# Centring x ahead of its transposes and applying its scale to the hidden sums, in a Fourier-mixing and MLP kernel

## The chip, the cores and the metric

The kernel runs on one core of a Trainium2 chip. The metric is the device time of one execution in microseconds (us), the median of several runs.

## What is computed

For x of 2048 rows (tokens) by 640 columns, a normalization and two branches that are summed with x:

```python
xn = layernorm(x)                                # over the 640 columns, eps 1e-5
a = xn @ dft_hid_re.T ; b = xn @ dft_hid_im.T    # 640 x 640
y = dft_seq_re @ a - dft_seq_im @ b              # 2048 x 2048
h = gelu(xn @ w1 + b1)                           # 640 -> 1536, tanh form
out = x + y + h @ w2 + b2                        # 1536 -> 640
```

All in float32. TensorE multiplies in a rounded float32 (`fp32r`), so each operand is split into a high part (rounded, by ScalarE) and a low part (the rest, by VectorE), and a product is three matmuls: high x high, high x low, low x high.

## The kernel before

The tokens are handled in four blocks of 512. The MLP of block 0 comes first, then that of blocks 1 and 2 together, then block 3, then the Fourier branch for all blocks. The order of each engine's instructions is written out by hand: the program's order is the queue's order on every engine, and each instruction waits only for the data and the places that it needs.

**The head** (lines 647 to 755). Four loads bring block 0's rows, a chunk of 128 rows each, into `row_places`. Meanwhile TensorE runs `NWARM` = 19 matmuls on zeros (line 666). The three tiles `warm` that they read have the places of the first three chunks of w1 (tag `w1r`), so a load of w1 waits until the warming matmuls on its tile are done: `NGATE` = (7, 10) says that the first tile is read by 7 of them, the second by 3, the third by the rest. Each chunk of x gets its mean and variance (chunk 1 on ScalarE, the others by `ln_stats` on VectorE), the reciprocal root by a Sqrt on ScalarE and a Newton step on VectorE (lines 690 to 713), and is normalized into `xp`: chunks 0 and 1 by ScalarE, 2 and 3 by VectorE in two parts. Then 20 transposes on TensorE (line 682) put block 0, transposed, in five PSUM banks, and five splits (line 736) make `XT`. With `XT` and the first w1 chunk's split the hidden sums of unit 0 start (line 320). `FIRST` is the order of unit 0's 15 matmuls.

**The units of block 0** (loop at line 1157). The 1536 hidden columns are 12 units of 128. `hidden(g)` is 15 matmuls that sum unit g in a PSUM bank, `unit` (line 332) its gelu on ScalarE, `split_unit` its split into `hs`, `output(g)` 15 matmuls that add its share to the output's five banks. Iteration i splits w1's chunk i+3 and w2's chunk i+1 (`prep_w1`, `prep_w2`; high on ScalarE, then low on VectorE), issues the loads of later chunks into the places so freed (three places each), then does `background(i)`, `hidden(i+2)`, `gelu(i+2)`, `late(i)` and `output(i)`. So TensorE's order is hidden(2), output(0), hidden(3), output(1) and so on.

**The rows beside the units.** Later stages need the normalized rows in other layouts. `background`, `late` and `normalize_a` compute statistics of blocks 1 and 2, normalize their rows in place on VectorE (`ln_apply`, line 231), and move them: `put_rows` writes them to DRAM (`xn`), `put_z` turns them around into `Z["b"]` (block 2, in the tile that `xp` had) and `Z["a"]` (block 1, in the place of block 0's rows), each by 16 DMAs; those of `Z["a"]` are all issued by POOL. `make_forms` then transposes parts of Z on VectorE and splits them. Loads are issued by SP in order. ScalarE's Sqrt and Gelu are in different tables, so a table load stands between them.

The lines that the change and the prediction speak of:

```python
W1[0], first_w1 = slots[1, 0], w1r.pop(0)...             # 722
nc.scalar.activation(W1[0][:, 0], first_w1, AF.Copy)      # 723
for i in range(NF - 2):                                   # 1157
    prep_w1(i + 3)
    if i == 3: normalize_a()
    prep_w2(i + 1)
    load_w1(i + 6); load_w2(i + 4)
    background(i)
    acc = hidden(i + 2)
    gelu(i + 2, acc)
    late(i)
    output(i)
```

Of the kernel before, what the change touches and what calls it, by code (L numbers as in the profile page):

```python
# [10 lines left out]
F32 = mybir.dt.float32  # L11
# [8 lines left out]
NWARM = 19  # L20
NGATE = (7, 10)
# [5 lines left out]
def kernel(  # L27
# [105 lines left out]
    ident = early.tile([P, P], F32, name="ident")  # L133
    es_r = ExitStack()
# [41 lines left out]
    def split(hi, lo, src, perm=False):  # L176
# [6 lines left out]
        low(l, s, h)  # L183
# [26 lines left out]
    def ln_stats(c):  # L210
        m = MV
# [6 lines left out]
    def ln_scale(n):  # L218

        m = MV[:, :n]  # L220
        ve, r, t = m[:, :, 2], m[:, :, 3], m[:, :, 4]
        nc.scalar.activation(r, m[:, :, 1], AF.Sqrt, bias=eps[:, 0:1])
        nc.vector.tensor_scalar(ve, m[:, :, 1], EPS, None, op0=ALU.add)
        nc.vector.reciprocal(r, r)
        nc.vector.scalar_tensor_tensor(t, r, -0.5, r, op0=ALU.mult, op1=ALU.mult)
        nc.vector.tensor_tensor(t, t, ve, op=ALU.mult)
        nc.vector.scalar_tensor_tensor(r, t, 1.5, r, op0=ALU.add, op1=ALU.mult)

    def ln_apply(c, eng=nc.vector):
        m = MV[:, slot[c]]  # L230
        eng.tensor_scalar(xt[c], xt[c], m[:, 0:1], m[:, 3:4], op0=ALU.subtract, op1=ALU.mult)

    def ln_apply_chunked(dst, c, j0=0, j1=ND):

        m = MV[:, slot[c]]
# [51 lines left out]
    def prep_w1(i, n=None):  # L287
        if i < NF:
            W1[i] = slots[1, i]
            split(W1[i][:, 0], W1[i][:, 1], w1r.pop(i if n is None else n).rearrange("p a b -> p (a b)"))  # L290

    def prep_w2(i):
        if i < NF:
            W2[i] = slots[2, i]
            split(W2[i][:, 0], W2[i][:, 1], w2r.pop(i), perm=True)
# [36 lines left out]
    def unit(g, acc, plus=None, a=None):  # L332
# [4 lines left out]
        if plus is not None:  # L337
            add(a, plus, acc)
            acc = a
        nc.scalar.activation(a, acc, AF.Gelu_apprx_tanh, bias=b1c[:, i : i + 1])  # L340
# [10 lines left out]
    FIRST = [(0, 0), (0, 2), (1, 0), (1, 2), (0, 1), (2, 0), (2, 2), (1, 1), (3, 0), (3, 2)]  # L351
    FIRST += [(2, 1), (4, 0), (4, 2), (3, 1), (4, 1)]
# [327 lines left out]
    def transpose_x(c, j0, j1):  # L680
# [5 lines left out]
    last = 1  # L686
    f, m = MV[:, 0], MV[:, last]
    root, step, shift = f[:, 3:4], f[:, 4:5], f[:, 5:6]
    ln_stats(0)
    nc.scalar.activation(root, f[:, 1:2], AF.Sqrt, bias=eps[:, 0:1])  # L690
    scratch = mr.tile([P, 2 * TB], F32, tag="hs", bufs=3, name="scratch")[:, :D]
    nc.scalar.activation(scratch, xt[last], AF.Copy, scale=-1.0 / D, accum_out=m[:, 5:6])
    nc.scalar.activation(
        chunked(xp[:, last]),
        xt[last].rearrange("p (q c i) -> p q c i", q=Q, i=B),
        AF.Identity,
        bias=m[:, 5:6],
    )
# [1058 lines left out]
```

## Time and profile before

| | |
|---|---|
| median of 3 runs | 851.65 us (851.21 to 852.05) |
| span of the profiled execution | 849.9 us |
| TensorE, matmuls | busy 841.9 us, 99% of the span, 3711 |
| VectorE | busy 686.7 us, 81% |
| ScalarE | busy 368.6 us, 43% |
| GpSimd | busy 67.7 us, 8% |
| the chain of work that ended last | TensorE 98%, DMA 1% |
| DMA | 166.53 MB, mean 196 GB/s |

The span runs from the first to the last instruction of one execution taken by the hardware profiler; the page states no other time for that execution. The timed runs lie around it: their median is 1.75 us above the span. In the rows below, PE is TensorE's matmuls, PEld its weight loads, DVE VectorE, ACT ScalarE, POOL GpSimd, and SPq the queue on which SP issues DMAs. A timeline row has the start in us, the duration in us, the engine, the source line, the operation, what is written and read, the shapes, and how many instructions are merged in the row; in brackets, how long the engine was idle before it and what ended the wait. A row of the chain has start, duration, engine, tile and line.

### The profile page before, as it was taken

The page shows a single profiled execution, that of the slowest core. Times are in us where ns is not written, and L with a number is a line of the kernel's source. Part 1 is how long each engine was busy: PE and PEld are TensorE (multiplying, and loading weights), DVE is VectorE, ACT ScalarE, POOL GpSimd, SP SyncE. Part 2 cuts the span into 40 slices and gives each one's busy share as a digit, 9 for nine tenths or more (in the row PEclk, how much of TensorE's full clock was granted, in tenths as well). Part 3 has the DMA queues.
Part 4 walks back from the last instruction along what each step waited for, and adds up shares of the span by engine and source line. Part 5 has one row for each costly group of instructions (what it writes and reads, how often), then busy time and mean ns, then how long its engine had stood idle before and what let it go on. Part 6 is the DMA issues. An engine that isn't in the chain of part 4 may idle for free.

```text
span 849.9 us, 10599 instructions
## 1 busy us (share of the span) xinstructions
PE 841.9 (99%) x3711; PEld 696.7 (82%) x3711; DVE 686.7 (81%) x909; ACT 368.6 (43%) x527; POOL 67.7 (8%) x116
## 2 busy tenths in 40 slices
PE   8999999999999999999999999999999999999997
PEld 7888888888888888888888888888888888888886
DVE  7979889767844778979978887889967998885687
ACT  7655666654453555443444344232323433323241
POOL 0440024222301000000000000000000000000002
PEclk9999999999999999999999999999999999999999
DMA  8995667878977897958744679763745799705464
GB/s 230 288 248 158 139 163 250 260 223 305 262 192 199 333 323 138 209 120 193 158 137 107 167 220 283 165 144 99 214 150 156 229 237 234 303 19 180 124 172 108
DMA packets 199141, 166.53 MB, mean 196 GB/s; under 512 B 61648, under 2 KB 170192, under 8 KB 198576
## 3 DMA queue, kind: packets, MB, share of 16 engines
q1 hardware_dynamic: 188320, 140.42, 62.7%
q0 software_dynamic: 7600, 24.91, 8.7%
q10 hardware_dynamic: 3168, 0.52, 0.3%
q8 instruction: 29, 0.48, 0.2%
q14 instruction: 24, 0.20, 0.1%
HBM read 115.75 MB, written 46.14 MB: 190 GB/s over the span
## 4 chain that ended last, share of the span: by engine, by line
PE 98%; DMA 1%; DVE 0%; ACT 0%; SPq 0%; issue 0%; ACTq 0%
PE banks L301 29%; PE banks L302 29%; PE banks L300 29%; PE banks L320 10%; DMA row<-in_A_x_dram 1%; PE banks L682 0%; DVE st L215 0%; ACT xp L714 0%; SPq L208 0%; DVE yo L1722 0%; DVE mv L216 0%; ACT mv L707 0%; DVE mv L708 0%; ACTq L707 0%
## 5 line engine op out<-in xcount | busy, mean ns | idle before, releaser
L186 ACT ACTIVATE as<-r 128x1024 fp32r<-128x1024 f32 x80 | 85.0, 1062 | 171.1 <-PE banks L302 150.4
L300 PE MATMUL banks<-as,xab 128*128 128x512 f32 x407 | 158.3, 389 | 0.0
L302 PE MATMUL banks<-as,xab 128*128 128x512 f32 x407 | 158.3, 389 | 0.0
L301 PE MATMUL banks<-as,xab 128*128 128x512 f32 x407 | 158.3, 389 | 0.0
L189 DVE TENSOR_TENSOR as<-r,as 128x1024 fp32r<-128x1024 f32 x80 | 97.2, 1215 | 38.1 <-ACT as L186 38.0
L301 PEld LDWEIGHTS banks<-as,xab 128*128 128x128 f32 x407 | 76.4, 188 | 15.9
L302 PEld LDWEIGHTS banks<-as,xab 128*128 128x128 f32 x407 | 76.4, 188 | 15.8
L300 PEld LDWEIGHTS banks<-as,xab 128*128 128x128 f32 x407 | 76.4, 188 | 15.8
L300 PE MATMUL banks<-as,xc 128*128 128x512 f32 x224 | 87.1, 389 | 0.0
L301 PE MATMUL banks<-as,xc 128*128 128x512 f32 x224 | 87.1, 389 | 0.0
L302 PE MATMUL banks<-as,xc 128*128 128x512 f32 x224 | 87.1, 389 | 0.0
L186 ACT ACTIVATE as<-rt 128x1024 fp32r<-128x1024 f32 x32 | 34.0, 1063 | 72.5 <-PE banks L302 57.9
L320 PE MATMUL banks<-xt,xab 128*128 128x512 f32 x240 | 56.8, 390 | 0.0
L189 DVE TENSOR_TENSOR hs<-ab,hs 128x512 fp32r<-128x512 f32 x36 | 24.7, 685 | 37.6 <-ACT hs L186 37.6
L320 PEld LDWEIGHTS banks<-xt,xab 128*128 128x128 f32 x240 | 45.0, 188 | 9.4
L301 PEld LDWEIGHTS banks<-as,xc 128*128 128x128 f32 x224 | 42.1, 188 | 8.8
L302 PEld LDWEIGHTS banks<-as,xc 128*128 128x128 f32 x224 | 42.0, 188 | 8.7
L300 PEld LDWEIGHTS banks<-as,xc 128*128 128x128 f32 x224 | 42.1, 188 | 8.7
L1280 POOL DMA_DIRECT2D out_dram<-u x4 | 2.6, 658 | 568.8 <-DVE u L463 568.8
L302 PE MATMUL banks<-hs,xc 128*128 128x512 f32 x120 | 46.7, 389 | 0.0
L300 PE MATMUL banks<-hs,xc 128*128 128x512 f32 x120 | 46.7, 389 | 0.0
L301 PE MATMUL banks<-hs,xc 128*128 128x512 f32 x120 | 46.7, 389 | 0.0
(240 smaller groups left out, 1678.9 us busy)
## 6 DMA issues: line engine op xcount, KB each, us to landing
raw<-in_A_dft_seq_re_dram SPq DMA_DIRECT2D x64, 256.0 KB, 5.4
raw<-in_A_dft_seq_im_dram SPq DMA_DIRECT2D x64, 256.0 KB, 5.1
w1r<-in_B_w_dram SPq DMA_DIRECT2D x144, 80.0 KB, 3.5
wit<-wst POOLq DMA_DIRECT2D x15, 384.0 KB, 4.2
wit<-wst POOLq DMA_DIRECT2D x20, 256.0 KB, 4.5
forms_ab<-xab SPq DMA_DIRECT2D x4, 1280.0 KB, 7.7
xab<-wit SPq DMA_DIRECT2D x13, 384.0 KB, 4.5
row<-xn SPq DMA_DIRECT2D x14, 320.0 KB, 5.3
```

Source lines behind the costliest of these rows:

```text
L186: nc.scalar.activation(h, s, AF.Copy)
L189: nc.vector.tensor_tensor(l, s, h.bitcast(F32), op=ALU.subtract)
L300: nc.tensor.matmul(acc, wh, mh, start=first, stop=False, skip_group_check=goes_on)
L301: nc.tensor.matmul(acc, wh, ml, start=False, stop=False, skip_group_check=goes_on)
L302: nc.tensor.matmul(acc, wl, mh, start=False, stop=last, skip_group_check=goes_on)
L320: nc.tensor.matmul(acc, W1[i][:, a, j * P : (j + 1) * P], XT[j][:, b], start=n == 0, stop=n == len(steps) - 1)
L1280: queues[q % len(queues)].dma_start(rows_of(out, t)[:, :, q * DQ + c0 : q * DQ + c1], src[q * B : (q + 1) * B])
```

## The change

Four things are done.

- The head: chunks of block 0 are only centred before the transposes (chunks 0, 2 and part of 3 on VectorE by `centre`, chunk 1 and part of 3 on ScalarE by `centre_beside`). Their scale (the reciprocal root) is computed behind the splits of `XT`. Four more transposes on TensorE spread the scale of each token over all partitions (bank 0), and ScalarE copies it to a tile `scale`. The gelu of each of the first 12 units is preceded by a product of the sums with `scale` on VectorE. 14 warming matmuls are left, with gates at 6 and 9, and the first w1 chunk's high part goes to VectorE.
- The rows of block 0 are scaled into `row_places` by ScalarE (`rows_beside`), those of block 2 normalized by ScalarE (`ln_apply_beside`).
- The low parts of w1's and w2's chunks are kept back (`rest`) and issued in `beside_split`, between the high and the low part of unit i+2's own split; the loads into the places that they free follow there, ahead of the normalization and the moves of the rows.
- Block 1 gets its statistics (in tile `MVA`) and normalization one iteration earlier, and the backgrounds from iteration 4 on stand behind the gelu; those of 6 and later move up by one or part of one.

```diff
-NWARM = 19
-NGATE = (7, 10)
+NWARM = 14
+NGATE = (6, 9)
...
+    def roots(m):
+        nc.scalar.activation(m[:, :, 3], m[:, :, 1], AF.Sqrt, bias=eps[:, 0:1])
...
+    def ln_apply_beside(c):
+        m = (MVA if 4 <= c < 8 else MV)[:, slot[c]]
+        nc.scalar.activation(xt[c], xt[c], AF.Identity, bias=m[:, 5:6], scale=m[:, 3:4])
...
+        if g < NF:
+            add(a, acc, scale, ALU.mult)
+            acc = a
         nc.scalar.activation(a, acc, AF.Gelu_apprx_tanh, bias=b1c[:, i : i + 1])
...
     ln_stats(0)
-    nc.scalar.activation(root, f[:, 1:2], AF.Sqrt, bias=eps[:, 0:1])
...
+    centre(0)
+    mean_beside(1)
+    centre_beside(1)
+    spread_beside(1)
+    ln_stats(2)
+    centre(2, 0, 2)
+    mean_beside(3)
+    centre(2, 2, ND)
+    nc.vector.tensor_scalar(MV[:, 3, 0:1], MV[:, 3, 5:6], -1.0, None, op0=ALU.mult)
+    centre_beside(3, 0, 2)
+    centre(3, 2, ND)
     transpose_x(0, 0, ND)
+    transpose_x(1, 0, ND)
     transpose_x(2, 0, 2)
     transpose_x(3, 0, 2)
-    transpose_x(last, 0, ND)
     transpose_x(2, 2, ND)
-    transpose_x(3, 2, ND - 1)
+    transpose_x(3, 2, ND)
+    W1[0], first_w1 = slots[1, 0], w1r.pop(0).rearrange("p a b -> p (a b)")
+    nc.vector.tensor_copy(W1[0][:, 0], first_w1)
...
-    acc0 = hidden(0, slice(1, None))
+    acc0 = hidden(0, slice(0, 14))
     prep_w1(1)
-    acc1 = hidden(1)
+    spread_beside(3)
+    v, r, t = MV[:, :, 1], MV[:, :, 3], MV[:, :, 4]
+    nc.scalar.activation(r, v, AF.Sqrt, bias=eps[:, 0:1])
...
+    prep_w1(2)
     prep_w2(0)
-    prep_w1(2)
+    acc1 = hidden(1, slice(0, 2))
+    hidden(0, slice(14, None))
+    hidden(1, slice(2, 6))
+    for c in range(NC):
+        nc.tensor.transpose(bank(0)[:, c * P : (c + 1) * P], MV[:, c, 3:4].to_broadcast([P, P]), ident)
+    hidden(1, slice(6, None))
+    scale = rows.tile([P, TB], F32, tag="yt", bufs=2, name="scale")
+    nc.scalar.activation(scale, bank(0), AF.Copy)
...
+    def beside_split(i, lows):
+
+        if i == 1:
+            ln_scale_table(MV)
+            ln_shift()
+        for f in lows:
+            f()
+        if i + 6 < NF + 3:
+            load_w1(i + 6)
+        load_w2(i + 4)
+        if i == 1:
             Z["b"] = zo_tile("z_b")
             for c in range(2 * NC, 3 * NC):
-                ln_apply(c)
+                ln_apply_beside(c)
             put_z(Z["b"], A["rows_b"], nc.gpsimd, nc.sync)
             put_rows(2, A["rows_b"])
         if i == 2:
-            ln_stats(6)
-            ln_stats(7)
+            ln_scale_table(MVA)
+            Z["a"] = as_z(row_places)
+            for c in range(NC, 2 * NC):
+                ln_apply(c)
+            put_z(Z["a"], A["rows_a"], nc.gpsimd)
...
     for i in range(NF - 2):
-        prep_w1(i + 3)
-        if i == 3:
-            normalize_a()
+        lows = []
+        prep_w1(i + 3, rest=lows)
...
-        prep_w2(i + 1)
-        if i + 6 < NF + 3:
-            load_w1(i + 6)
-        load_w2(i + 4)
-        background(i)
+        prep_w2(i + 1, lows)
+        rows_beside(i)
+        if i < 4:
+            background(i)
         acc = hidden(i + 2)
...
-        gelu(i + 2, acc)
+        gelu(i + 2, acc, lambda k: beside_split(i, lows) if k else None)
+        if i >= 4:
+            background(i)
         late(i)
         output(i)
```

In `background`, what stood under iteration 6 (moves of block 1's rows, the forms `ua0`, `ua1`, `va0`, a difference in `Z["b"]`) stands under 5, `oa0` and `va1` under 6 instead of 7, the next difference and two transposes under 7 instead of 8, and the loads of x's rows for block 0's output and of b2 under 9 instead of 8.

More of the change, by code (lines that the diff above doesn't have):

```diff
@@ L133 @@
     ident = early.tile([P, P], F32, name="ident")
+    MVA = early.tile([P, 4, 6], F32, name="mva")
     es_r = ExitStack()
@@ L182, in split @@
         high(h, s)
-        low(l, s, h)
+        if rest is None:
+            low(l, s, h)
+        else:
+            rest.append(lambda: low(l, s, h))
     def high(h, s):
```

154 lines of the change are left out of this document (74 added, 80 removed).

## The prediction

> **What bounds the kernel now.** I read the page first (busy shares), then the chain of work that ended last, then the timeline of the first 25 us engine by engine, and last the timeline and the waits of 25 to 70 us.
>
> ```profile
> PE 841.9 (99%) x3711; PEld 696.7 (82%) x3711; DVE 686.7 (81%) x909; ACT 368.6 (43%) x527; POOL 67.7 (8%) x116
> ```
>
> ```profile
> 9.71 2.27 PE banks L682 x19
> ...
> 12.32 10.07 PE banks L320 x44
> 22.39 0.23 PE banks L300
> ...
> 25.79 3.40 PE banks L320 x15
> ...
> 32.59 3.40 PE banks L320 x15
> ```
>
> The span is 849.9 us and TensorE is busy for 841.9 of it. From 9.71 us to the output's last steps the chain holds nothing but matmuls: one unit of the MLP (15 matmuls of the hidden sums, 15 of the output) takes 32.59 - 25.79 = 6.80 us, or 0.227 us a matmul, and none waits. So the loop cannot get shorter by other engines' work; only its start can move. The most that can be won is in front of 9.71; all that can be lost is a new wait.
>
> ```profile
> 1.92 7.05 PE L666 MATMUL banks<-warm 128*128 128x512 f32 x19 [1.92 <-DVE warm L657]
> 9.71 2.27 PE L682 MATMUL banks<-ident,xp 128*128 128x128 f32 x19 [0.73 <-ACT xp L714]
> 11.73 0.48 PE L320 MATMUL banks<-xt,xab 128*128 128x512 f32 x1
> 12.04 0.27 PE L682 MATMUL banks<-ident,xp 128*128 128x128 f32 x1
> 12.07 10.32 PE L320 MATMUL banks<-xt,xab 128*128 128x512 f32 x44
> 22.23 0.39 PE L300 MATMUL banks<-hs,xc 128*128 128x512 f32 x1
> ```
>
> Nineteen warming matmuls, 20 transposes of x, 45 hidden matmuls, and the first output matmul at 22.23. **That last time is the one I forecast**; behind it the order of TensorE is unchanged.
>
> **The change, part by part. 1: the head.** The transposes no longer wait for the roots, only for the means.
>
> ```profile
> 4.66 0.21 DVE L216 BATCH_NORM_AGGREGATE mv<-st 128x2 f32<-128x12 f32 x1
> 5.10 0.72 ACT L692 ACTIVATE scratch<-row 128x640 f32<-128x640 f32 x1
> 5.73 0.18 ACT L692 ACTIVATION_READ_ACCUMULATOR scratch<-row 128x1 f32 x1
> 5.95 0.83 ACT L693 ACTIVATE xp<-row,mv 128x640 f32<-128x640 f32 x1
> 6.81 0.74 ACT L699 ACTIVATE scratch<-xp 128x640 f32<-128x640 f32 x1
> 7.28 0.83 DVE L215 BATCH_NORM_STATS2 st<-row 128x6 f32<-128x320 f32 x2
> 9.60 1.51 DVE L236 TENSOR_SCALAR xp<-row,mv 128x256 f32<-128x256 f32 x4
> 11.03 2.56 ACT L186 ACTIVATE xt<-banks 128x512 fp32r<-128x512 f32 x5
> 11.83 3.07 DVE L189 TENSOR_TENSOR xt<-banks,xt 128x512 fp32r<-128x512 f32 x5
> ...
> 14.82 0.81 DVE L189 TENSOR_TENSOR xab<-w1r,xab 128x640 fp32r<-128x640 f32 x1
> ```
>
> Chunk 0: its statistics end at 4.87 as now. Centring is the instruction of L236 with one operand less; four halves took 1.51, so a whole chunk about 0.6 (bounds 0.4 and 0.82, the pass over two tensors at 14.82): ready 5.5. Chunk 1: ScalarE no longer does the root first, so it starts when the chunk lands, by 5.10 at the latest; I take 4.7. Mean, centring and spread take 0.85 + 0.86 + 0.8 and end at about 7.2. Chunk 3 has landed by 7.28, since its statistics start then; its mean on ScalarE ends at 8.0 to 8.1, two of its five blocks are centred there in 0.5 (between two fifths of L693's 0.83 and the whole) by 8.5, the rest on VectorE by 8.8. Now TensorE:
>
> ```profile
> 2.51 0.63 PE L666 MATMUL banks<-warm 128*128 128x512 f32 x1
> ...
> 4.22 0.63 PE L666 MATMUL banks<-warm 128*128 128x512 f32 x1
> 4.65 0.63 PE L666 MATMUL banks<-warm 128*128 128x512 f32 x1
> ...
> 7.19 0.62 PE L666 MATMUL banks<-warm 128*128 128x512 f32 x2
> 7.43 0.62 PE L666 MATMUL banks<-warm 128*128 128x512 f32 x2
> 7.65 0.63 PE L666 MATMUL banks<-warm 128*128 128x512 f32 x2
> ...
> 10.72 0.38 PE L682 MATMUL banks<-ident,xp 128*128 128x128 f32 x2
> ```
>
> The warming matmuls start 0.43 apart up to the 13th at 7.19 (eleven steps behind the second, at 2.51) and 0.23 apart after it: there the clock doubles, although the column of the granted clock reads 1.00 throughout. The 14th of them starts at 7.43, so the first transpose can follow at 7.66. At 0.11 each (the 10th of the 19 started at 10.72, about 1.0 behind the first) the 20 transposes run to 9.86, none of them waiting: the 13th, the first of chunk 3, is due at 8.98 with its data ready at 8.5. The present one of that kind started at 10.72, and the split of block 0 on ScalarE followed at 11.03, the first hidden matmul at 11.73: 1.01 behind the transpose. So the first hidden matmul comes at 8.98 + 1.01 = **10.0 instead of 11.73**.
>
> The first chunk of w1 must be there:
>
> ```profile
> 5.31 5.60 SPq L278 DMA_DIRECT2D w1r<-in_B_w_dram  x12
> ```
>
> ```profile
> w1r<-in_B_w_dram SPq DMA_DIRECT2D x4, 80.0 KB, 2.1
> ```
>
> Its first load waits for the gate's 7th warming matmul (4.65 + 0.63 = 5.28); with the 6th it is issued 0.43 earlier, at 4.88. Four issues at about 0.45 and 2.1 to 2.2 to land (the second row, the loads issued from 6.3 to 8) give 8.4. VectorE, free at 8.7, rounds it (0.5; bounds 0.4 and 0.82, as for the centring) and takes the low part (0.82) by 10.1: in time for the third matmul.
>
> From 10.0 to the first output matmul: 45 matmuls x 0.227 = 10.2; a wait of 0.25 at the second, since its block is split 0.48 after the first (L186); four transposes of the scale, 0.44 at the 0.11 of L682 (bounds 0.44 and 0.9, if a broadcast operand streams at half speed); and 0.19 that today's 10.50 us holds beyond its 45 matmuls and its one visible transpose. Together 21.1. **The head gives 22.23 - 21.1 = 1.15 us.**
>
> The four scale transposes wait for the roots of all chunks. Behind the splits of x ScalarE does w1's next high part, chunk 3's spread and one root (to 13.5), VectorE a low part and four small steps (to 14.6); TensorE gets there at 15.2. Nothing waits. The copy of the scale ends at 16.4.
>
> **2: the units.** Each of the first 12 gets one more VectorE pass, and the low parts of the next weights go behind it. The weights' low part used to be done an iteration ahead; now it starts only when the hidden sums before it end, and is needed 3.40 + 0.45 us later.
>
> ```profile
> 16.95 0.69 ACT L340 ACTIVATE ab<-banks,b1c 128x512 f32<-128x512 f32 x1
> 17.68 0.63 ACT L186 ACTIVATE hs<-ab 128x512 fp32r<-128x512 f32 x1
> 24.84 8.23 SPq L278 DMA_DIRECT2D w1r<-in_B_w_dram  x8
> 30.60 1.28 ACT L222 ACT_TABLE_LOAD   x1
> 42.95 2.18 DVE L231 TENSOR_SCALAR rt<-rt,mv 128x640 f32<-128x640 f32 x4
> ```
>
> ```profile
> L463 DVE TENSOR_TENSOR ab<-ab,banks 128x512 f32<-128x512 f32 x7 | 4.8, 684 | 3.8 <-PE banks L302 3.8
> ```
>
> The product costs 0.68, in sequence 0.61 (L189's five in 3.07); 12 of them are 7.3 us of VectorE, against four row passes (2.2, the row at 42.95) that go to ScalarE at L693's 0.83 or 0.75 in sequence. A chunk's statistics take 0.83 + 0.21, a high part of weights 0.63 in sequence, as L692's pass of 640 columns. With hidden(3) starting at 21.1 + 3.4 = 24.5, the nearest points are:
> - hidden(3): ScalarE from 16.4: table 1.3, two units 2.6, so VectorE splits unit 1 until 21.0; two statistics (2.1), product 0.61, low part 0.82: 24.5 plus 0.15 to reach TensorE, needed at 24.95. Spare 0.3.
> - hidden(5): ScalarE adds two weight pairs (2.5), four rows (3.0), unit 2 (1.3), two tables and two roots (2.9), unit 3 (1.4): 31.4. VectorE then splits unit 3 (to 32.1), four statistics to 36.2, product and low part to 37.7; needed at 38.55. Spare 0.7. Behind it two further low and small steps and four row passes end at 41.3.
> - hidden(9): next.
>
> Each costs nothing while spared; an error of half a microsecond in such a sum costs TensorE that half, once. The loads of w1 and w2 wait for these low parts, which end later in the unit than now; but SP is at earlier loads until 33.1 (the row at 24.84) when the low part that frees the next place ends at about 31, so I price that at nothing. Without the cover such a load would land some 2 us later, and it is used three units, 20 us, after its issue.
>
> **3: the rows' moves.** Block 1's rows are normalized by 41.3, and POOL moves them.
>
> ```profile
> 45.43 3.81 POOL L762 DMA_DIRECT2D row<-rt  x7 [2.76 <-DVE rt L231]
> ```
>
> ```profile
> 62.69 1.30 DVE L259 STREAM_TRANSPOSE ztua<-row 128x512 f32<-128x512 f32 x2 [1.05 <-DMA row<-rt]
> ...
> 67.98 0.69 DVE L189 TENSOR_TENSOR hs<-ab,hs 128x512 fp32r<-128x512 f32 x1
> ```
>
> Now the rows are done at 45.13, POOL issues from 45.43, VectorE waits for the landing until 62.69, 17.26 behind the first issue, and is free again 5.29 later, at 67.98. The forms stand one iteration earlier after the change, in front of the product and the low part for hidden(9). That matmul group starts at 24.5 + 6 x 6.8 = 65.3, its low part is needed at 65.6: landing + 5.29 + 0.61 + 0.82 = landing + 6.72, so the rows must land by **58.9**. First issue at 41.6 and the same 17.26 give 58.9: no wait, and no spare.
>
> **Sum:** 1.15 won, nothing lost: the span 849.9 becomes 848.75. The median of the timed runs, 851.65, lies 1.75 above the span; carried over, **850.5 us**.
>
> **The rivals.**
> *A, the rows land late.* Each microsecond beyond 58.9 is a microsecond of TensorE. For it: 16 issues on POOL overlap block 2's moves more than now. Against: they start 3.8 earlier. If they land no earlier than now, at 62.69, hidden(9) waits 3.8, and the time is 850.5 + 3.8 = 854.3. From 60.05 on the gain is gone. This is the case on the slower side. Chance 0.15.
> *B, the clock.* The clock doubled 5.27 us behind the first matmul (1.92 to 7.19), and 14 at 0.43 last only 6.0. If in an execution the doubling comes later and the transposes do not bring it, the 20 transposes take 4.4 instead of 2.2, and up to 12 hidden matmuls 0.2 more each: 1.15 turns into a loss of 0.3 + 2.2 + 2.4 - 1.15 = 3.75, 855.4; if it comes half-way, 0.4 to 1.2 are lost and the time is 850.9 to 851.7. The present rows only show the clock kept through 2.3 us of transposes, not raised by them. Chance 0.08 for the whole, 0.12 for half. The Trainium skill speaks for B: its page "TensorE: Matmul & The Clock Gate" says in "Part 4: PE-mode transpose" that transposes do not count as busy time for the clock, and in Part 1 that the activity window is free-running, so the doubling moves between executions.
> *C, small waits.* A third to one microsecond lost in hidden(3) to hidden(5), where 0.3 to 0.7 is spared, or in a first w1 chunk that lands at 9.5 instead of 8.4 (0.5): 850.8 to 851.5. Chance 0.25.
> *D, more than forecast.* If the clock doubles early, the transposes wait for chunk 3 alone (8.6), the first hidden matmul comes at 9.65: 850.1. Nothing in front of 9.71 offers more, so over 0.2% (1.7 us) is nearly excluded.
>
> **How the numbers follow.** Forecast 0.40 (with D), A 0.15, B 0.20, C 0.25. The range leaves out the far parts of A (0.05), B whole (0.08) and the end of D (0.06): 849.9 to 853.0. Faster by over 0.2% means below 849.95: 0.07, D at its end. Slower means above 853.35: A from 61.75 on and B whole, 0.15. Within 0.2%, about what a measurement of this kernel can tell: 0.78.
>
> **What would show it.** The first hidden matmul at 10.0 and the first output matmul at 21.1; four transposes there without a wait in front; no idle TensorE at hidden(3), (5) and (9); the first transpose of block 1's form at 58.9 or sooner; warming matmuls whose spacing halves before the 14th. An idle TensorE behind 25 us names A or C, transposes 0.22 apart name B.

## The result and the profile after

| | before | changed |
|---|---|---|
| median | 851.61 us (851.21 to 852.19, 12 runs) | 853.21 us (851.64 to 857.39, 12 runs) |
| span of the profiled execution | 849.9 us | 850.1 us |
| time of that execution | about 852.0 us (span and 2.1) | 852.21 us |

The ratio is 1.0026, with a 95% interval of 1.0013 to 1.0038: the changed kernel is slower by a quarter of a per cent, and its executions spread over 5.8 us where before's spread over 1. The profiled executions whose time is known lie 1.9 to 2.2 us above their spans, most of them 2.1. The execution profiled is one of the faster ones, so its trace shows the cause, but not the typical size.

TensorE's timeline of the changed kernel (columns as before; line 331 is the hidden sums, 311 to 313 the output, 696 the transposes, 772 those of the scale):

```profile
1.92 6.22 PE L680 MATMUL banks<-warm 128*128 128x512 f32 x14 [1.92 <-DVE warm L671]
7.98 2.46 PE L696 MATMUL banks<-ident,xp 128*128 128x128 f32 x20
10.37 5.31 PE L331 MATMUL banks<-xt,xab 128*128 128x512 f32 x21
15.52 0.60 PE L772 MATMUL banks<-ident,mv 128*128 128x128 f32 x4
...
21.43 0.39 PE L311 MATMUL banks<-hs,xc 128*128 128x512 f32 x1
...
65.63 0.61 PE L331 MATMUL banks<-xt,as 128*128 128x512 f32 x2
66.92 3.24 PE L331 MATMUL banks<-xt,as 128*128 128x512 f32 x13 [0.68 <-DVE as L193]
```

The first output matmul comes at 21.43 instead of 22.23: the head gained 0.80. Every unit keeps that lead up to hidden(9) at 65.63. There the third matmul should start at 65.63 + 2 x 0.227 = 66.08 and starts at 66.92: 0.84 lost, and 0.13 more in the rest of the group. The lead of 0.80 becomes a lag of 0.17, and the span is 0.2 longer. The page of waits has only this one and the start of the warming:

```profile
PE banks L680 <- DVE warm L671: 1.9, 1, 1.9
PE banks L331 <- DVE as L193: 0.7, 1, 0.7
```

What TensorE waited for is the low part of w1's chunk. VectorE's timeline shows what stood in front of it:

```profile
39.45 2.35 DVE L235 TENSOR_SCALAR rt<-rt,mva 128x640 f32<-128x640 f32 x4
...
58.04 0.69 DVE L193 TENSOR_TENSOR hs<-ab,hs 128x512 fp32r<-128x512 f32 x1
60.16 1.30 DVE L270 STREAM_TRANSPOSE ztua<-row 128x512 f32<-128x512 f32 x2 [1.43 <-DMA row<-rt]
61.57 0.69 DVE L193 TENSOR_TENSOR xab<-ztua,xab 128x512 fp32r<-128x512 f32 x1
...
64.32 1.22 DVE L477 TENSOR_TENSOR z_b<-z_b,row 128x1024 f32<-128x1024 f32 x1
65.45 0.69 DVE L477 TENSOR_TENSOR ab<-banks,scale 128x512 f32<-128x512 f32 x1
66.05 0.81 DVE L193 TENSOR_TENSOR as<-w1r,as 128x640 fp32r<-128x640 f32 x1
...
82.52 1.22 DVE L477 TENSOR_TENSOR row<-row,z_b 128x1024 f32<-128x1024 f32 x1
84.57 0.83 DVE L193 TENSOR_TENSOR w1f<-w1r,w1f 128x640 fp32r<-128x640 f32 x1 [0.84 <-ACT w1f L190]
```

The first row is the normalization of block 1's rows. VectorE idles 1.43 us until these rows have landed, and from 60.16 to 83.7 it waits for nothing: forms, products, low parts, one behind the other. A late landing shifts the whole stretch. How the rows were moved is on GpSimd's queue, first before's, then the changed kernel's:

```profile
40.44 2.22 POOL L770 DMA_DIRECT2D xn<-r  x4 [0.19 <-issue]
45.43 3.81 POOL L762 DMA_DIRECT2D row<-rt  x7 [2.76 <-DVE rt L231]
```

```profile
35.49 4.36 POOL L784 DMA_DIRECT2D z_b<-r  x8 [7.96 <-ACT r L242]
39.84 2.18 POOL L792 DMA_DIRECT2D xn<-r  x4
42.09 2.18 POOL L784 DMA_DIRECT2D row<-rt  x4
45.17 0.55 POOL L784 DMA_DIRECT2D row<-rt  x1 [0.90 <-DMA xn<-r]
46.61 0.55 POOL L784 DMA_DIRECT2D row<-rt  x1 [0.88 <-DMA xn<-r]
47.87 0.55 POOL L784 DMA_DIRECT2D row<-rt  x1 [0.71 <-DMA xn<-r]
49.37 4.89 POOL L784 DMA_DIRECT2D row<-rt  x9 [0.94 <-DMA xn<-r]
```

Before, GpSimd was done with the four writes of block 2's rows (`xn<-r`) at 42.66 and idled 2.76 until block 1's rows were ready. Now the rows are ready earlier, and the moves stand directly behind the writes. In this execution the first move is not late for that: it comes at 42.09, 0.29 behind the end of the normalization (41.80), as before (0.30, from 45.13 to 45.43). But each of the 5th to 8th waits 0.7 to 0.9 for the landing of a write, eight places ahead of it.

### The profile page after: what moved, and what is told of

Same layout as the page of the kernel before. It is cut to its first block, busy times and chain, and to the rows that moved or that the text cites. A ratio compares the mean times of both kernels' runs of the same rounds, so it can differ in the third digit from the quotient of the medians.

```text
span 850.1 us, 10606 instructions
## 1 busy us (share of the span) xinstructions
PE 842.2 (99%) x3710; PEld 696.1 (82%) x3710; DVE 688.6 (81%) x905; ACT 375.5 (44%) x538; POOL 67.8 (8%) x116
## 4 chain that ended last, share of the span: by engine, by line
PE 93%; ACT 2%; DMA 2%; POOL 1%; issue 1%; DVE 1%; ACTq 0%; DVEq 0%
PE banks L312 29%; PE banks L311 29%; PE banks L313 28%; PE banks L331 7%; DMA xn<-r 1%; DMA row<-rt 1%; PE banks L680 1%; POOL z_b L784 1%; POOL row L784 0%; ACT r L242 0%; ACT row L800 0%; ACT xab L190 0%; PE banks L696 0%; ACT ab L354 0%; POOL xn L792 0%
```

## The experiments

The theories are named in the expectations. **Theory 1**: the clock after the short warming. **Theory 2**: block 1's rows land late. **Theory 3**, formed after the second run: VectorE has no slack behind the landing, because the change gave each of the first 12 units a product.

### The warming: 19 and 10 matmuls, and 14 in the kernel before

```diff
-NWARM = 14
+NWARM = 19
```

> The changed kernel with 19 warming matmuls instead of 14, gates unchanged. Theory 1 (clock): the spread of the changed kernel's runs (spans 849.5 to 855.3 us) comes from executions in which the clock doubles after the 14 warming matmuls are over. With 19 the doubling always falls into them: the warming ends at about 8.9, the first hidden matmul comes at about 11.2, the first output matmul at about 22.2, the wait at hidden(9) shrinks from 0.84 to 0.1 or nothing, and the times lie within 1 us of each other, median 851.4 to 852.0. Theory 2 (late moves): the spread comes from the landing of block 1's rows, which holds up hidden(9) by 1 us in one execution and by several in another. Then the times still spread over several us, the upper ones some 0.8 us below those of the changed kernel.

854.79 us (853.13 to 856.25, 5 runs; ratio 1.0035, 1.0023 to 1.0047). The first output matmul came at 21.72; the rows' first transpose at 61.93, and hidden(9) waited 2.30. The wait did not shrink, and the spread of 3.1 us did not go: theory 1's numbers missed.

```diff
-NWARM = 14
-NGATE = (6, 9)
+NWARM = 10
+NGATE = (6, 8)
```

> The changed kernel with 10 warming matmuls (gates 6 and 8). They end at about 6.4, before any doubling that was seen. Theory 1 (clock): the transposes run 0.22 apart, the hidden matmuls 0.43 apart until the doubling comes, and nearly every execution is slow: 854 to 858. If the transposes bring the doubling, hidden matmuls are at full speed and the time is that of the changed kernel's best runs, 851.6 to 852.5. Theory 2 (late moves): as the changed kernel, median 852 to 853.5, since the transposes are then held by the third chunk of x at 8.9 and nothing else changes.

852.54 us (851.47 to 857.53, 5 runs; ratio 1.0032, 1.0010 to 1.0054): three executions at 851.5 to 852.5, two at 856.6 and 857.5. In the profiled one the head gained 1.45, the rows' transpose started at 59.75, and hidden(9) waited 1.08. VectorE did not wait for the rows there, but for ScalarE, and ScalarE for a load of w2:

```profile
57.09 0.74 ACT L190 ACTIVATE r<-w2r 128x640 fp32r<-128x640 f32 x1 [1.85 <-DMA w2r<-in_B_w_dram]
```

Into the kernel before:

```diff
-NWARM = 19
-NGATE = (7, 10)
+NWARM = 14
+NGATE = (6, 9)
```

> The kernel before with 14 warming matmuls and gates at 6 and 9, nothing else. TensorE is then idle from about 8.0 to 9.71. Theory 1 (clock): in some executions the doubling has not come when the warming ends; transposes 0.22 apart and hidden matmuls 0.43 apart follow, 2 to 5 us are lost, and the times spread from 851.3 to 857, median over 852.3. Theory 2 (late moves): the moves are those of before, so the times stay at 851.2 to 852.2.

851.69 us (851.25 to 855.07, 12 runs; ratio 1.0008, 0.9999 to 1.0017). Nine executions lie at 851.2 to 852.0, three at 854.0 to 855.1, and these three have a mean granted clock of 0.996 to 0.997 where the nine have 0.998 to 0.999. In the profiled one, among the nine, the warming ended early and TensorE idled 2.42 us before its first transpose. That a short warming with a long wait behind it costs 3 us in single executions is likely from the clocks, but none of the three was profiled. In the changed kernel the transposes follow at once, and with 19 warmings its spread stayed; theory 1 did not explain it.

### Block 1's forms put back

```diff
-        if i == 5:
+        if i == 6:
             put_rows(1, A["rows_a"], nc.sync)
```

and the forms and subtractions behind it in iterations 6, 7 and 8, as before.

> The changed kernel with block 1's forms, and the steps behind them, back in the iterations where the kernel before had them (6, 7, 8 instead of 5, 6, 7, 8). Both theories: no wait for the rows in front of hidden(9), so the profiled execution has no idle TensorE there and gains 0.8 to 1.0. Theory 1 (clock): the spread stays, from about 850.7 to 856.5, median about 852.2. Theory 2 (late moves): the spread goes, all times within 1 us, median about 850.8.

853.44 us (852.82 to 853.70, 11 runs; ratio 1.0019, 1.0010 to 1.0028). The spread shrank from 5.8 to 0.9, which is theory 2's; the level did not fall, which is not. TensorE's timeline of this kernel, in the first pair:

```profile
104.61 0.47 PE L311 MATMUL banks<-as,w1f 128*128 128x512 f32 x1 [1.51 <-DVE zc L477]
```

Hidden(9) no longer waits, but hidden(11) loses 0.35 and the first pair 1.67 in all, for VectorE's last sum. This led to theory 3.

### The moves ahead of the writes

```diff
-            put_rows(2, A["rows_b"])
         if i == 2:
...
             put_z(Z["a"], A["rows_a"], nc.gpsimd)
+            put_rows(2, A["rows_a"])
```

> The changed kernel with the order of two groups of transfers on GpSimd's queue swapped: the 16 moves of block 1's rows go ahead of the 4 that write block 2's rows back to DRAM (so as to have the same order of buffers, the 4 behind them write block 1's rows in place of block 2's: that part of the output is not what the reference has, the work of every engine is the same). In the changed kernel the 5th to 8th move wait 0.90, 0.88, 0.71 and 0.94 us for those writes. Theory 2 (the moves land late): the first move is issued at about 40 instead of 42.1, the rows have landed by 57.5 to 58.5, hidden(9) has no idle time (0.84 + 0.13 in the changed kernel), and the median is about 0.9 below the changed kernel's in the same job, without executions above 855. Theory 1 (the clock after the short warming): hidden(9)'s wait may go, but the spread stays, some executions above 855. Theory 3 (VectorE's queue as a whole: each unit got a product more, and the weights' low parts wait behind it): the wait at hidden(9) goes and comes back later, in hidden(10), hidden(11) or in the first pair, 0.1 to 1.7 us, as with the forms put back.

**851.24 us** (850.50 to 851.72, 11 runs; ratio 0.9990, 0.9982 to 0.9999). GpSimd's queue and VectorE's timeline of this kernel:

```profile
34.96 4.34 POOL L784 DMA_DIRECT2D z_b<-r  x8 [7.97 <-ACT r L242]
41.48 6.51 POOL L784 DMA_DIRECT2D row<-rt  x12 [2.18 <-DVE rt L235]
48.35 0.55 POOL L784 DMA_DIRECT2D row<-rt  x1 [0.36 <-DMA row<-rt]
```

```profile
58.12 1.30 DVE L270 STREAM_TRANSPOSE ztua<-row 128x512 f32<-128x512 f32 x2
```

The first move is again issued 0.30 behind the normalization, but now twelve go without a wait, and VectorE finds the rows landed at 58.12. The writes behind them carry block 1's rows, so block 2's are left out of `xn`. TensorE waits nowhere behind its start: theory 2's expectation for the wait and the spread came true, theory 3's (a wait that comes back later) did not. The profiled span is 848.6, the forecast's 848.75 within 0.15, in one of the faster executions; by the medians of this job the kernel gains 0.69, by the ratio's interval 0.1 to 1.5, and 1.15 was forecast. So with the rows there in time the rest of the change is worth about what was forecast.

The same with 19 warming matmuls (`NWARM = 19`):

> The kernel with GpSimd's two groups swapped (851.24, no idle time at hidden(9); its 4 writes carry block 1's rows in place of block 2's) with 19 warming matmuls as before instead of 14. It isolates the warming, since nothing else moves in that kernel. Theory 2: the warming ends at 8.4 to 9.0 instead of 7.4 to 8.0, so the first hidden matmul comes 0.2 to 1.0 later: 851.5 to 852.2, spread as with 14. Theory 1 (the short warming costs single executions): median about that of 14 or lower, the spread smaller than its 1.2 us.

852.06 us (851.43 to 853.09, 11 runs; ratio 1.0005, 0.9996 to 1.0014), 0.8 above 14 warmings in another job. In the profiled execution, one of the slower ones (852.77), the first output matmul came at 21.64 instead of 20.89, block 1's transpose at 60.67 instead of 58.12, and hidden(9) waited 1.13:

```profile
42.23 6.51 POOL L784 DMA_DIRECT2D row<-rt  x12 [2.18 <-DVE rt L235]
```

```profile
60.67 1.30 DVE L270 STREAM_TRANSPOSE ztua<-row 128x512 f32<-128x512 f32 x2 [1.72 <-DMA xn<-rt]
```

The transpose reads the moved rows, although the profile names a write behind the moves as the last DMA to land. Twelve moves went without a wait here too, and yet the transpose started 18.44 behind the first of them, against 16.64 or less with 14 warmings. So the order on GpSimd's queue is not all that decides when the rows are there; what else does is not shown. The 14 warmings do not cause the spread, and 19 cost their 0.75.

### A low part ahead of the forms

```diff
+        if i != 6:
             prep_w1(i + 3, rest=lows)
...
+        if i == 5:
+            prep_w1(9)
         if i >= 4:
             background(i)
```

> The changed kernel with one split moved: the high and low part of w1's chunk for hidden(9) are made in iteration 5 behind the gelu's split, ahead of block 1's forms, which wait for the rows; all else as in the changed kernel, the output is the reference's. Theory 2 (the rows land late, and hidden(9) waits because its weights' low part stands behind the wait for them): the low part ends by 60, hidden(9) has no idle time whenever the rows land up to 3 us later, the executions above 855 go, and the median is 0.9 to 1.7 below the changed kernel's: 851.3 to 850.5 where before has 851.6. Theory 1 (clock): spread as in the changed kernel. Theory 3 (VectorE's queue as a whole): 0.1 to 1.7 us come back at hidden(10), hidden(11) or in the first pair, and the median stays at 852 to 853.5.

> The kernel of the run before with 18 warming matmuls instead of 14. Theory 1 (clock): the executions above 855 that are left with 14 go; otherwise the two kernels differ by the 0 to 0.7 us by which four more matmuls at 0.21 hold up the transposes. Theory 2: no difference in the spread. Where both act: this is the fastest of the four, 850.5 to 851.3.

> The changed kernel unchanged, as the measure for the three others on the same chip, and for a second profile of it. All theories: a median of 852.2 to 853.5 with single executions up to 857; hidden(9) idle for 0.8 us or more; if its profile is of a slow execution, theory 2 expects the excess as a longer wait at hidden(9), theory 1 as transposes and first matmuls at double duration, theory 3 as waits behind 70 us.

With the low part ahead 852.37 us (850.96 to 853.60, 12 runs; ratio 1.0005, 0.9997 to 1.0013), with 18 warmings besides 852.43 (851.31 to 854.30, 12 runs; 1.0008, 1.0000 to 1.0017), the changed kernel again 854.05 (851.45 to 857.02, 12 runs; 1.0029, 1.0017 to 1.0042). So the edit wins back 1.68 of the 2.12 us that the changed kernel is above before in this job, and four more warmings change nothing. The changed kernel's profiled execution was its fastest this time (851.45), with a wait of 0.44 at hidden(9). With the low part ahead the slowest of the 12 was profiled (853.60), and TensorE's timeline says where its time went:

```profile
73.95 3.25 PE L331 MATMUL banks<-xt,as 128*128 128x512 f32 x13 [0.59 <-DVE as L193]
...
81.75 3.28 PE L331 MATMUL banks<-xt,as 128*128 128x512 f32 x13 [0.70 <-DVE as L193]
```

The forms started at 61.82, hidden(9) did not wait, but hidden(10) and hidden(11) did, for the next low parts in the same stretch: theory 3's answer.

### The writes elsewhere

On SyncE (`put_rows(2, A["rows_b"], nc.sync)`), then on SyncE an iteration later, then on GpSimd behind the moves with the right rows:

> The changed kernel with the 4 writes of block 2's rows issued by SyncE, behind its 8 moves of block 2, instead of by GpSimd; the output is the reference's. GpSimd's 16 moves of block 1 follow its 8 moves of block 2 at once. If the places in GpSimd's queue held the rows up (each issue from the 5th waits for the landing of a write 8 places ahead): first issue at 41.5, the first stream transpose of block 1's form by 58.2 as with the two groups swapped, no idle time at hidden(9), the spread gone, and a median of 851.0 to 851.4, 0.5 to 0.9 below before's. If it was the traffic of the writes themselves, which now run beside the moves on another queue: the transpose at 59 to 60.5, 0.5 to 1.3 idle at hidden(9), 852 to 853. On SyncE w1's and w2's next loads stand behind the writes, some 2 to 4 us later; they are used 20 us after their issue, so this costs nothing, or, if it does, idle time at hidden(6) to hidden(8) with w1r or w2r as what it waits for.

> The changed kernel with the 4 writes of block 2's rows on SyncE, one iteration later than in the run with the writes on SyncE, so behind that iteration's loads of w1 and w2, which took 6.75 us to issue there with the writes in front and 2.02 with the two groups swapped; the output is the reference's. Theory 2, as it stands now (hidden(9) is late when either block 1's rows or the raw weights for hidden(8) and hidden(9) are held up by the writes of block 2's rows): the loads are issued at 41.6 to 43.7, the writes at 44 to 48, landed by 55, ahead of the split that takes their buffer at about 56; the form's first transpose by 59, hidden(9) idle for at most 0.5, the median 851.0 to 851.8 and no execution above 854. If the writes slow down the moves and the loads by their traffic wherever they run: the loads of the next iteration or the moves take 5 us or more, 1 to 2 idle at hidden(9), 852.5 to 855.

> The changed kernel with the 4 writes of block 2's rows left on GpSimd but issued behind the 16 moves of block 1, now of the right rows; the output is the reference's. The buffer of block 2's rows is taken over by chunks of w2, whose split then waits for these writes, issued at 51 to 55 and landed by 57 to 60. If only the order on GpSimd's queue matters: as with the groups swapped, no idle time at hidden(9), 851.0 to 851.4. If the buffer is needed before 57: ScalarE waits for the writes in front of w2's high part, the gelu behind it comes late, and TensorE idles 1 to 4 us at an output group between 50 and 70 us: 852.5 to 855.

In that order 854.57 us (853.83 to 856.83, 5 runs; ratio 1.0035, 1.0023 to 1.0048), 853.04 (852.43 to 854.09, 11 runs; 1.0018, 1.0009 to 1.0026) and 858.53 (856.77 to 858.81, 5 runs; 1.0073, 1.0059 to 1.0087): in none did the case with no wait at hidden(9) come, and the third is slower than its other case said. SyncE's queue in the first:

```profile
42.12 4.36 SPq L792 DMA_DIRECT2D xn<-r  x4
46.60 6.75 SPq L289 DMA_DIRECT2D w1r<-in_B_w_dram  x4
```

The four loads of w1 behind the writes took 6.75 us to issue, against 2.02 with the groups swapped. That alone is not new, since in the profile after the same loads took 6.97 with the writes on GpSimd; but here they begin at 46.60 instead of 43.94. ScalarE then waited 2.00 for one of them, VectorE for ScalarE, and hidden(9) waited 1.69. In the second, ScalarE's split of w2's chunk into the buffer that the writes read started after a wait of 1.63, in the third after 5.93; the profile names other DMAs as the last to come there, so that the writes held it up is inferred from the buffer. TensorE lost 0.85 and 5.14 there. In all three VectorE was held up by ScalarE's splits and not by block 1's rows: moving the writes moved the delay.

### The low parts ahead, and the work taken from VectorE

```diff
+        if not 5 < i <= 8:
             prep_w1(i + 3, rest=lows)
...
+        if 5 <= i <= 7:
+            prep_w1(i + 4)
         if i >= 4:
             background(i)
```

> The changed kernel with w1's splits for hidden(9), hidden(10) and hidden(11) all made an iteration earlier, in iterations 5, 6 and 7 behind the gelu's split and ahead of the forms; the output is the reference's. In the changed kernel VectorE works without a gap from 60.2, where the rows have landed, to 83.7, and these three low parts stand in that stretch behind forms that nothing needs before the first pair at 103 us. Theory 2 with theory 3 (the landing shifts this whole stretch, and TensorE sees the shift at the first low part in it): no idle time at hidden(9), hidden(10) and hidden(11) even if the rows land at 62; the head's 0.5 to 1.5 us stay won up to the pairs; median 850.8 to 851.5, spread below 2 us; at most 0.2 to 0.5 idle in the first pair. If the traffic alone decides (raw weights late as well): idle time of 0.5 to 2 at hidden(9) or at an output group, on ScalarE's high part, and 852 to 853.5.

854.22 us (852.57 to 855.85, 6 runs; ratio 1.0035, 1.0023 to 1.0046). Its waits:

```profile
PE banks L680 <- DVE warm L671: 1.9, 1, 1.9
PE banks L311 <- DVE zc L477: 1.5, 1, 1.5
PE banks L313 <- DVE w1f L193: 0.3, 1, 0.3
```

No hidden group waits, although the forms started at 61.03; but 0.44 is lost at 87 us, and the wait is back at the end of VectorE's queue, in the first pair, the same 1.5 as with the forms put back. The order on VectorE decides where TensorE waits, not whether. Theory 3's own expectation for this run, 850.8 to 851.5, was too hopeful by 3.

The same kernel without the added products in units 8 to 11:

```diff
-        if g < NF:
+        if g < 8:
             add(a, acc, scale, ALU.mult)
```

> The kernel of the run before (w1's splits for hidden(9) to hidden(11) ahead of the forms) without the product of the scale and the hidden sums in units 8 to 11: that part of the computation is left out, so those four units are not scaled. It takes 4 x 0.61 us from VectorE between 60 and 88 us, and nothing from any transfer. Theory 3 (from the landing of block 1's rows on VectorE has no slack until the first pair, and the added products used up what there was): the 1.5 us that TensorE waited for VectorE's last sum at 105 go, since 2.4 us less stand in front of it, and the 0.44 at 87; median 851.2 to 852.2, spread below 1.5 us. Theory 2 (the landing alone, whatever VectorE has to do after it): the wait at 105 stays above 0.8 and the median above 853.

**850.68 us** (850.35 to 851.08, 11 runs; ratio 0.9987, 0.9978 to 0.9996). The rows' first transpose started at 60.30, two microseconds later than with the moves swapped, and yet:

```profile
PE banks L680 <- DVE warm L671: 1.9, 1, 1.9
```

TensorE waits nowhere, and the spread is 0.7; what the kernel leaves out is the scale of those four units. The forms also started 0.73 earlier than in the run before, which is less than the 2.2 us that TensorE lost there. So four products, 2.4 us of VectorE, decide here. VectorE's busy time from 60 to 110 us says the same, in the order before, changed, and this kernel (length, then PE, PEld, DVE, ACT, POOL busy with counts, granted clock, DMA):

```profile
60.00:110.00 50.00, 50.00 (x223) 41.39 (x222) 43.19 (x68) 29.86 (x51) 1.13 (x2) 1.00 0.65 152
```

```profile
60.00:110.00 50.00, 49.32 (x218) 40.42 (x217) 45.81 (x72) 30.88 (x51) 1.13 (x2) 1.00 0.61 148
```

```profile
60.00:110.00 50.00, 50.00 (x222) 41.39 (x221) 43.95 (x69) 30.53 (x51) 1.12 (x2) 1.00 0.63 150
```

43.19, 45.81 and 43.95 of 50 us: the change put 2.6 us more on VectorE there, and without the four products 0.8 of it is left.

Last, with the product left in, four subtractions moved from VectorE to GpSimd (`nc.gpsimd.tensor_tensor` in place of `add` in iterations 5, 7 and 8), in the changed kernel and in the one with the low parts ahead:

> The changed kernel with the four subtractions of blocks in iterations 5, 7 and 8 (128x1024, 1.22 us each on VectorE) on GpSimd, which has nothing to do there; the output is the reference's. Theory 3: VectorE has 1.22 us less ahead of the low part for hidden(9) and 4.9 less up to the first pair; hidden(9) waits only when the rows land after 60.2, no wait later; median 850.9 to 851.8, below before's by up to 0.7 or equal to it. Theory 2: hidden(9)'s wait falls by 1.2 as well, so both give the same here; they part in the next run. If GpSimd's passes hold up VectorE's (a slower VectorE beside them): its passes of 1.22, 0.69 and 0.82 us beside a subtraction are longer, and 0.5 to 2 us are lost again.

> The four subtractions on GpSimd, and w1's splits for hidden(9) to hidden(11) ahead of the forms; the output is the reference's. Theory 3: no idle time of TensorE from the first hidden matmul to the pairs and none at 87 or 105, even with the rows at 62; the head's gain of 0.5 to 1.5 us is kept: median 850.4 to 851.2, below before's, spread below 1.5 us. Theory 2 (the landing alone): 852 or more with a wait somewhere between 65 and 106 us.

860.62 us (856.71 to 861.67, 5 runs; ratio 1.0096, 1.0081 to 1.0112) and 856.69 (855.20 to 859.27, 6 runs; 1.0060, 1.0049 to 1.0072): both theories' numbers missed, and the third case that the first expectation names happened, larger than it said. GpSimd's timeline of the second, then VectorE's:

```profile
63.25 2.41 POOL L833 TENSOR_TENSOR z_b<-z_b,row 128x1024 f32<-128x1024 f32 x1 [7.78 <-DMA w1r<-in_B_w_dram]
65.74 2.74 POOL L843 TENSOR_TENSOR z_b<-z_b 128x1024 f32<-128x1024 f32 x1
68.55 2.68 POOL L840 TENSOR_TENSOR row<-z_b,row 128x1024 f32<-128x1024 f32 x1
```

```profile
64.14 2.07 DVE L193 TENSOR_TENSOR xab<-ztua,xab 128x512 fp32r<-128x512 f32 x1
66.25 0.71 DVE L270 STREAM_TRANSPOSE ztva<-row 128x512 f32<-128x512 f32 x1
66.88 2.15 DVE L193 TENSOR_TENSOR xab<-ztua,xab 128x512 fp32r<-128x512 f32 x1
68.95 2.83 DVE L193 TENSOR_TENSOR xab<-ztva,xab 128x512 fp32r<-128x512 f32 x1
71.71 0.68 DVE L477 TENSOR_TENSOR ab<-banks,scale 128x512 f32<-128x512 f32 x1
```

A low part that takes 0.65 to 0.69 alone takes 2.1 to 2.9 beside a subtraction on GpSimd; the transpose keeps its 0.71. So these two runs say nothing on the theories. The Trainium skill, page "SBUF — State Buffer", section "Who interferes with whom", says that a VectorE instruction with two SBUF inputs contends with a GpSimd instruction that reads SBUF; these rows agree, 0.69 becoming 2.07.

## Why the prediction was wrong, point by point

The forecast was 850.5, in a range of 849.9 to 853.0; measured were 853.21, slower than before where a gain was forecast.

- **The head was right.** Forecast: first output matmul at 21.1, 1.15 won. The twelve profiled kernels with the changed head and 14 warmings give 20.75 to 21.75, mean 21.13. In the profile after, the 14 warmings ran 0.43 apart to the end (rival B's case in part) and 0.35 of the gain was missing: the first hidden matmul at 10.37 instead of 10.0. In others the clock doubled earlier (14 in 5.6 us) and up to 1.48 was won (rival D). An early doubling did not always help: in the one with 21.75, 14 warmings took 5.44 us, and TensorE then waited 0.8 for ScalarE's centring. The four transposes of the scale had no wait in front.
- **Hidden(3) and hidden(5) were right.** No wait there; rival C did not come in the changed kernel.
- **The deadline at hidden(9) was right.** "Landing + 6.72", needed by 58.9. In the profile after the low part runs from 66.05 to 66.86, and the matmul starts at 66.92, 6.76 behind the transpose's start at 60.16; it was due at 66.08, so the forms had to start by 59.32 in this execution. The same 6.76, with each kernel's own lead of the head (22.23 minus its first output matmul), gives for the other kernels with VectorE's work in the changed order (the last column says what held VectorE up ahead of the transpose: the rows, or a split on ScalarE that had waited for a DMA):

| kernel | transpose starts | head's lead | wait by the sum | wait seen | held up by |
|---|---|---|---|---|---|
| moves swapped | 58.12 | 1.34 | none | none | nothing |
| changed, again | 59.23 | 1.33 | 0.44 | 0.44 | rows |
| writes on SyncE, later | 59.62 | 1.36 | 0.86 | 0.85 | split of w2 |
| 10 warmings | 59.75 | 1.45 | 1.08 | 1.08 | split of w2 |
| swapped, 19 warmings | 60.67 | 0.59 | 1.14 | 1.13 | rows |
| writes on SyncE | 60.85 | 0.96 | 1.69 | 1.69 | split of w1 |
| 19 warmings | 61.93 | 0.51 | 2.32 | 2.30 | rows |
| writes behind the moves | 64.00 | 1.28 | 5.16 | 5.14 | split of w2 |

So the loss at TensorE follows from when VectorE starts block 1's forms, whatever held them up.

- **The step that failed** is "First issue at 41.6 and the same 17.26 give 58.9: no wait, and no spare." In the profile after, the first issue came at 42.09 and the transpose at 60.16. The 0.5 at the start is little loss, since the head was 0.35 later than forecast and the deadline moved with it, to 59.32; the transpose came 18.07 behind the issue, and the 0.81 above 17.26 is the wait of 0.84. That latency was carried over from moves that no write preceded closely. In the seven other profiles with the writes in front in which VectorE waited for the rows, it was 17.30 to 20.85. There the start failed too: the first issue came at 41.61 to 44.63, in five of the seven 0.6 to 1.6 later than 0.3 behind the normalization, because GpSimd was still at block 2's moves and writes (before's own trace has it at these writes until 42.66). Rival A names these moves; the sum has no term for them. Swapped, with the issue at 41.48 and the transpose at 58.12, the step's number was even undercut, but with 19 warmings that order gave 18.44. So the writes ahead of the moves are part of the delay, and the whole of it stays open.
- **The second failure** is that the ledger ended there ("hidden(9): next") and that rival A thus priced one wait, once. The products were counted up to hidden(5) and in hidden(9)'s sum, not in the queue behind it. Before, the transpose started at 62.69 and nothing waited; with four products more, 61.0 is too late in either order.
- **Rival A was the case.** Its place, and its price of one for one, are what the traces show, although with 10 warmings and with the writes on SyncE raw weights, and not the rows, were late. Its point of no gain, 60.05, is the profiled execution's 60.16 within 0.1, with the head's lead at 0.80: the sum puts the deadline at 66.08 - 6.76 = 59.32, and 0.80 behind it the lead is gone. A chance of 0.15 for a step that had "no spare", and whose latency came from another order of transfers, was too small; the whole range had to lean upward.
- **Its end at 854.3 was too low.** Four of the changed kernel's 12 executions lie above 855. They raise its median only from 852.7 to 853.2: the other eight are 1.1 above before too. Most of the 12 are slower than the profiled one, so they probably waited longer than its 0.84; none of them was profiled. In the run of the changed kernel again, the six executions up to 853.5 have a mean granted clock of 0.998 to 0.999, the six from 854.6 to 857.0 one of 0.996 to 0.997. Where a longer wait was profiled, the clock fell. TensorE of the kernel with subtractions on GpSimd and low parts ahead, which waited from 69.25 to 73.17 (columns as above, the granted clock third from the right):

```profile
66.00:70.00 4.00, 3.40 (x16) 2.48 (x14) 3.97 (x4) 1.26 (x2) 3.92 (x2) 1.00 0.95 267
70.00:74.00 4.00, 0.83 (x2) 0.73 (x3) 3.28 (x4) 1.55 (x3) 1.24 (x1) 0.72 0.29 79
74.00:78.00 4.00, 4.00 (x10) 3.07 (x10) 3.90 (x5) 2.28 (x4) 1.42 (x1) 0.50 0.50 148
78.00:82.00 4.00, 4.00 (x18) 3.23 (x17) 3.44 (x4) 1.23 (x2) 0.96 (x1) 0.92 0.06 16
```

  Behind the wait of 3.92, 13 matmuls take 5.60 us (73.17 to 78.77) instead of 13 x 0.227 = 2.95. A single wait of 2.1 (19 warmings) showed no such fall; two of 2.1 with two matmuls between them (writes behind the moves) did. As an estimate, a mean of 0.996 instead of 0.9985 is 850 x 0.0025 / 0.5 = 4.2 us at half clock, so about 2 us of loss. That rows landing at 62 or later cause these executions is argued, not shown: no execution of the changed kernel above 855 was profiled. Where the wait at hidden(9) is gone (forms put back, moves swapped, low part ahead with 14 and with 18 warmings, all three low parts ahead, products left out), no execution has a mean clock below 0.998. But two of six with all three low parts ahead still lie at 855.8: a long time does not need the fall of the clock. The Trainium skill, page "TensorE: Matmul & The Clock Gate", Part 1, puts the fall at an idle window of about 3.4 us; the wait of 3.92 and the single one of 2.1 agree, and the two of 2.1 last longer than that together.
- **The loads, priced at nothing**, were not always free: with 10 warmings ScalarE waited 1.85 for one of w2, with the writes on SyncE 2.00 for one of w1, and hidden(9) came late behind these. In the profile after, four of them took 6.97 us to issue from 43.94, and no wait of TensorE followed. In how many of the unprofiled executions the loads were late, and not the rows, is not known.
- **The carry of 1.75** between span and median was too small: 2.1 lies between a span and its own execution, and before's profiled one was 0.4 above its median. With 2.1 the forecast would have been 850.85. The 0.4 may lie in before's head: with 14 warmings its first output matmul came at 21.69 instead of 22.23, in a span of 849.4. Then the head had less to win over the median than 1.15, as the 0.69 with the moves swapped suggests; that is argued, not shown.

What stays open is a version with the whole computation that keeps the head's 1.15: of the edits tried, the one low part ahead comes nearest (852.37), and none beats the kernel before.

## What to carry to other kernels

When a step is moved forward, its start is the latest of all queues it passes, the issuing engine's own backlog included: read that queue's rows in the old trace. And a latency measured behind other neighbours is carried over as a range (here 17.26 became 17.3 to 20.9), not as one number. A small pass added to every unit is paid where its engine already works without a gap, so look for the longest gapless stretch behind the change and add the passes there; reordering within that stretch only moves the wait. And a sum that comes out at "no spare" belongs in the range with its whole far side, since a wait at TensorE of a few microseconds can cost the clock as well.

## What the runs showed of the hardware

A subtraction of 128x1024 takes 2.4 to 2.7 us on GpSimd against 1.22 on VectorE, and VectorE's passes with two SBUF inputs beside it take 2.1 to 2.9 instead of 0.69. The clock's doubling in the warming moves between executions: 14 warming matmuls took 4.88 us (14 in the kernel before), 5.60 (forms put back) and 6.22 (the profile after). Behind a wait of 3.9 us TensorE ran at half clock for 5.6 us. Four loads of w1 on SyncE took 6.97 us to issue where four writes of rows had been issued before them on GpSimd, 6.75 with these writes ahead on SyncE itself, and 2.02 where the writes came later.
